# A planner's 1,870 priorities replaced, and its formula for matmul durations rewritten

## The chip, the core and the metric

The kernel runs on one core of a Trainium2 chip. The metric is the device time of one execution in microseconds (us); the time before is the median of three runs. A profile is one further execution, taken by the hardware profiler. "PE" is TensorE's matmuls, "PEld" its weight loads, "DVE" VectorE, "ACT" ScalarE, "POOL" GpSimd, "SP" the engine whose queue issues most of the DMAs.

## The reference, cut to what matters

The input `x` has 2048 rows and 512 columns. Two branches of it are mixed by a gate for each row:

```python
g = sigmoid((x * gate_w).sum(-1, keepdims=True))
a = irfft2(rfft2(x) * (w_r + 1j * w_i), s=(2048, 512))      # spectral filter
b = gelu(x @ w1 + b1) @ w2 + b2                             # 512 -> 1792 -> 512
return g * a + (1 - g) * b
```

All of it is in single precision.

## The kernel before, in words

Every matrix product is split for accuracy: an operand is rounded to a high part (`...h`, type fp32r) and a rest (`...l`), and a product is the sum of high by high, high by low and low by high. ACT makes most high parts, DVE subtracts to get the low parts, and PE runs the products.

The 2048 rows are 16 blocks of 128. `forward(j)` treats one block of the spectral branch: DVE folds the block (tiles `eo`, `cl`), ACT and DVE split it (`eoh`, `eol`), PE multiplies it with a table of cosines and sines (`pd`), ACT and DVE split what comes out (`x..h`, `x..l`), PE transforms along the rows of the block (`py`), and the result stays in SBUF as `y`. The PE steps of `pd` are runs of two matmuls: two with 260 columns for the high part and two with 130 columns for the low part (`prod`, lines 716 to 735). Butterflies between blocks (`radix4`), the filter (`filt`) and the way back (`stage4`, `inverse`) follow. In `inverse` the PE steps of `pz` mix matmuls of 256 and of 128 columns, and `pa` has runs of 256 columns.

The dense branch, `mlp(half, c)`, runs for two halves of the 14 groups of hidden units and four groups `c` of 512 rows: `up` gives `ph` (12 matmuls of 512 columns a step), ACT applies the gelu, the result is split (`g_..h`, `g_..l`), and `down` adds up `po` (3 matmuls a step, 512 columns, or 256 in the very last output group). This branch is 1,344 products of 512 columns, 33 of them divided into two of 256, and is most of PE's work.

Nothing in this program runs in the order in which the Python text names it. Every operation is first entered as a step of a `Graph` with its engine, a planned duration, a planned delay until its result is seen (`lag`), and a rank. `Graph.schedule()` (lines 219 to 339) then simulates the engines with these durations. Whenever an engine is free in that simulation, it takes, of the steps whose inputs are there and whose buffers can be had, the one with the lowest rank. It never leaves an engine idle because of a rank alone, with one exception: DVE and ACT may hold back up to 0.35 us for a step of lower rank that is about to be ready (`AHEAD`). Buffers of one class are handed out in a fixed sequence (`takes`, lines 244 to 255), whatever the ranks are. A PE step whose input comes from another engine is held back by another 0.4 us in the plan (`SPARE`, line 116). At most 8 DMAs of the SP queue (`hw`) and 3 of the POOL queue (`ring`) are under way at a time. The order that comes out is the order in which each engine's instructions are emitted, and each engine's instructions are executed in that order, with semaphores between engines. The planned times themselves are not used on the chip.

The ranks are a list of 1,870 numbers, `RANKS` (lines 342 to 452), in hundredths of a planned microsecond, one for each step: 470 on PE, 691 on DVE, 452 on ACT, 207 on the SP queue, 50 on the POOL queue. The planned duration of a PE step of `k` matmuls is `c_pe(n, k)` (line 494), where the caller gives the column count `n`.

The first PE step is `warm` (line 595 and after), eleven products of zeros before the data are there. The last steps are the second half's outputs for `c == 2`: `last` (lines 1164 to 1177) scales the last two `po` sums on DVE (line 1168), combines them with the spectral result (line 1173) and sends them off (line 1176). Just before it, `inverse(1, 1)` gives its result through `od` (line 999), `uv` (line 1002) and `y` (lines 1021 and 1024).

Of the kernel before, what the change touches and what calls it, by code (L numbers as in the profile page):

```python
# [172 lines left out]
class Graph:  # L173
# [282 lines left out]
def tile_kernel(ctx: ExitStack, tc: tile.TileContext, xt, w1, w2, b1, b2, x0g, wf, wrev, out, consts):  # L456
# [37 lines left out]
    def c_pe(n, k=1):  # L494
        return k * (n / 2400 + 0.0135) + 0.005
# [8 lines left out]
    def m(emit, n, k, reads, writes, rank=BULK):  # L504
        return add("pe", c_pe(n, k), 0.25, emit, reads, writes, rank)
# [785 lines left out]
```

## Time and profile before

| | |
|---|---|
| time, median of 3 runs | 372.75 us (372.29 to 372.97) |
| span of the profiled execution, first to last instruction | 370.8 us |
| PE busy | 365.1 us (98%), 1,838 matmuls |
| DVE busy | 327.5 us (88%), 691 instructions |
| ACT busy | 229.6 us (62%), 454 instructions |
| DMA moved | 62.99 MB |

The profiled execution's span is 1.95 us below the median time of the runs. What lies around the span, before the first and after the last instruction, is in the time of the runs and not in the span; the same 1.95 us is added wherever a span is turned into a time below.

A busy PE is an engine on which some matmul is under way; matmuls overlap, so that the duration of one is longer than the distance from its start to the start of the next. The pace of PE is read from those distances. "Idle before" is the time an engine stood still before an instruction, and the arrow names what ended it.

### The profile page before, as it was taken

What the parts mean: (1) busy time and instruction counts of PE and PEld (TensorE: products, weight loads), DVE (VectorE), ACT (ScalarE), POOL (GpSimd) and SP (SyncE); (2) the same over time, 40 slices, a digit from 0 to 9 for tenths busy, and PEclk for the clock granted to TensorE, in tenths of its full rate; (3) what the DMA queues carried; (4) which work ended last, traced back from release to release, by engine and by line L of the source; (5) the groups of instructions that cost most, each with busy time, mean ns of one, the idle gap of its engine ahead of it and who ended that gap; (6) DMA issues with size and microseconds to landing.
All of it is one profiled execution on the core that took longest, in us unless ns stands there. A gap on an engine that the chain in (4) does not pass through costs nothing.

```text
span 370.8 us, 5565 instructions
## 1 busy us (share of the span) xinstructions
PE 365.1 (98%) x1838; PEld 309.9 (84%) x1838; DVE 327.5 (88%) x691; ACT 229.6 (62%) x454; POOL 44.1 (12%) x54
## 2 busy tenths in 40 slices
PE   8999999999999999999999999999999999999995
PEld 6888888888888888888888888888888888888885
DVE  4999999999999789999999999588849696789996
ACT  5776587976678735375367213894697549457830
POOL 0000000000000002021032020001403222221031
PEclk9999999999999999999999999999999999999999
DMA  8962899425954216479289762318968999736268
GB/s 276 389 194 73 257 282 342 147 71 151 289 173 141 77 23 170 142 157 256 72 214 267 225 120 55 57 25 291 209 130 112 211 285 187 130 88 139 88 85 198
DMA packets 50868, 62.99 MB, mean 170 GB/s; under 512 B 4656, under 2 KB 31344, under 8 KB 50064
## 3 DMA queue, kind: packets, MB, share of 16 engines
q1 hardware_dynamic: 43496, 49.54, 41.3%
q0 software_dynamic: 7200, 12.85, 23.1%
q8 instruction: 14, 0.23, 0.2%
q10 hardware_dynamic: 144, 0.26, 0.2%
q14 instruction: 14, 0.11, 0.1%
HBM read 38.64 MB, written 23.73 MB: 168 GB/s over the span
## 4 chain that ended last, share of the span: by engine, by line
PE 95%; DVE 1%; DMA 1%; issue 0%; ACT 0%; SPq 0%; DVEq 0%
PE ph L530 41%; PE po L530 40%; PE pz L530 4%; PE pd L530 4%; PE py L530 3%; PE pa L530 3%; DMA xr<-in_xt 1%; DVE uv L1002 0%; DVE y L1021 0%; SPq L588 0%; DVE y L1024 0%; DVE mxl L650 0%; DVE o L1168 0%; ACT mxh L649 0%; ACT od L999 0%
## 5 line engine op out<-in xcount | busy, mean ns | idle before, releaser
L1106 ACT ACTIVATE ph<-ph,b1t 128x512 f32<-128x512 f32 x56 | 36.9, 659 | 41.5 <-PE ph L530 39.9
L949 ACT ACTIVATE sw<-y,al 64x512 f32<-64x512 f32 x32 | 23.0, 722 | 2.2 <-DVE y L812 1.6
L908 DVE TENSOR_TENSOR m<-y,wf 128x514 f32<-128x514 f32 x32 | 20.8, 689 | 0.2
L956 DVE SCALAR_TENSOR_TENSOR pq<-y,al,sw 128x256 f32<-128x256 f32 x32 | 14.4, 481 | 5.9 <-ACT sw L952 5.5
L521 POOL DMA_DIRECT2D bacc<-o x12 | 10.5, 877 | 73.2 <-ACT o L1155 60.2
L521 POOL DMA_DIRECT2D wa7l<-in_w x1 | 1.0, 1017 | 141.0 <-ACT wa7l L582 141.0
L1155 ACT ACTIVATE o<-po 128x512 f32<-128x512 f32 x12 | 7.1, 595 | 15.9 <-PE po L530 15.8
L1152 ACT ACTIVATE o<-po,b2t 128x512 f32<-128x512 f32 x16 | 10.7, 686 | 7.6 <-PE po L530 7.5
L1002 DVE TENSOR_TENSOR uv<-pa,od 128x512 f32<-128x512 f32 x16 | 10.6, 685 | 3.6 <-ACT od L999 3.5
L764 ACT ACTIVATE y<-pys 64x257 f32<-64x257 f32 x24 | 10.0, 418 | 5.2 <-DVE pys L761 4.8
L530 PE MATMUL pd<-cf,eoh 128*128 128x260 f32 x64 | 12.7, 285 | 0.0
L688 DVE TENSOR_TENSOR eo<-xr 128x256 f32<-128x256 f32 x30 | 12.0, 418 | 0.0
L530 PEld LDWEIGHTS pd<-cf,eoh 128*128 128x128 f32 x64 | 10.6, 189 | 1.5 <-issue 0.2
L999 ACT ACTIVATE od<-pa 128x512 f32<-128x512 f32 x8 | 4.8, 599 | 10.2 <-PE pa L530 9.9
L952 ACT ACTIVATE sw<-y 1x512 f32<-1x512 f32 x16 | 10.1, 629 | 0.4
L530 PE MATMUL pd<-cf,eol 128*128 128x130 f32 x64 | 10.3, 253 | 0.0
L702 DVE TENSOR_TENSOR xr<-eo 128x256 f32<-128x256 f32 x24 | 9.8, 418 | 0.1
L530 PEld LDWEIGHTS pd<-cf,eol 128*128 128x128 f32 x64 | 9.6, 189 | 0.1
L649 ACT ACTIVATE mxh<-xm 128x512 fp32r<-128x512 f32 x12 | 6.9, 623 | 3.7 <-PE ph L530 3.7
L650 DVE TENSOR_TENSOR mxl<-xm,mxh 128x512 fp32r<-128x512 f32 x12 | 7.8, 686 | 1.2 <-ACT mxh L649 1.2
L705 DVE TENSOR_TENSOR eol<-xr,eoh 128x512 fp32r<-128x512 f32 x12 | 8.3, 688 | 0.2
L1046 DVE SCALAR_TENSOR_TENSOR ba<-gb,ba 128x512 f32<-128x512 f32 x12 | 8.1, 685 | 0.3 <-DMA ba<-bacc 0.3
(713 smaller groups left out, 1353.6 us busy)
## 6 DMA issues: line engine op xcount, KB each, us to landing
wf<-in_wf SPq DMA_DIRECT2D x16, 257.0 KB, 4.9
bacc<-o SPq DMA_DIRECT2D x16, 256.0 KB, 3.3
xr<-in_xt SPq DMA_DIRECT2D x15, 256.0 KB, 3.5
war<-in_w SPq DMA_DIRECT2D x14, 256.0 KB, 3.5
wbr<-in_w SPq DMA_DIRECT2D x14, 256.0 KB, 3.5
xm<-in_xt SPq DMA_DIRECT2D x12, 256.0 KB, 4.3
bacc<-o POOLq DMA_DIRECT2D x12, 256.0 KB, 4.0
ba<-bacc SPq DMA_DIRECT2D x12, 256.0 KB, 3.2
```

The source lines that it names most:

```text
L521: return add("pool", kb / 150, 3.4, lambda: nc.gpsimd.dma_start(dst(), src(), accum_op=ALU.add), reads, writes, rank)
L530: pe.matmul(ps, w, x, start=start, stop=stop)
L688: v(lambda s=s, op=op: vec.tensor_tensor(eo.ap()[:, s], x.ap()[:, 0:2], x.ap()[:, 2:4], op=op), 256, [x], [(eo, s)], FEED)
L702: v(lambda k=k, op=op: vec.tensor_tensor(quarter(cl, k), eo.ap()[:, :, 0], eo.ap()[:, :, 1], op=op), 256, [eo], [(cl, k)] if j % 4 == 0 or ...
L764: a(lambda o=o, i=i: act.activation(Y[j].ap()[o:o + HP, 1], pys.ap()[i:i + HP, 1], AF.Copy), 257, [(pys, 1)], [(Y[j], 1 + k)], 0, more=0.1)
L908: v(lambda mk=mk, k=k, y=y, w=w: vec.tensor_tensor(mk.ap(), y.ap(), w.ap()[:, k:k + 1, :ND].to_broadcast([P, 2, ND]), op=ALU.mult), 514, [ ...
L949: a(lambda sw=sw, y=y, o=o, i=i: act.activation(sw.ap()[o:o + HP], y.ap()[i:i + HP, ::-1, :HD], AF.Copy, scale=al.ap()[i:i + HP, 0:1]), 51 ...
L952: a(lambda sw=sw, y=y, j=j: act.activation(sw.ap()[HP:HP + 1], y.ap()[HP:HP + 1, ::-1, :HD], AF.Copy, scale=math.cos(math.pi * j / NJ)), 5 ...
L956: v(lambda sw=sw, pq_=pq_, y=y, j=j, k=k, op=op: vec.scalar_tensor_tensor(pq_.ap()[:, k], y.ap()[:, k, :HD], al.ap()[:, 1 + j:2 + j], sw.a ...
L1002: v(lambda i=i, op=op: vec.tensor_tensor(uv.ap()[:, :, i], ps.ap()[:, 0], od.ap(), op=op), 512, [ps, od], [(uv, i)], 2)
L1106: a(lambda f=f, ps=ps: act.activation(ps.ap(), ps.ap(), AF.Gelu_apprx_tanh, bias=b1t.ap()[:, f:f + 1]), 600, [b1t], [ps], 0.9 if half else ...
L1152: a(lambda o=o, ps=ps, q=q: act.activation(o.ap(), ps.ap(), AF.Identity, scale=-1.0, bias=b2t.ap()[:, q:q + 1]), 600, [b2t, ps], [o])
```

## The change

`RANKS` gets 1,870 other numbers, and `c_pe` another formula. No step is added or removed, no step's instructions are changed, and buffers, their counts, the lags and the other engines' planned durations stay as they are. The order that `Graph.schedule()` works out from the new ranks and durations is a new one on all engines and queues, DMAs included.

```diff
 RANKS = (
-    -149, 43, 217, 3, 143, 100, 150, 574, 1118, 447, 437, 885, 624, 1856, 1001, 866, 832, 912, 1753, 1799, 1869, 396,
-    517, 392, 844, 2523, 2641, 2614, 2664, 2689, 2749, 3018, 2746, 2717, 2784, 3053, 2805, 2960, 3278, 3147, 3324, 3185,
...
+    1739, 333, 416, -261, 178, -1542, -1584, 475, 1315, 602, 458, 538, 1168, 2342, 1590, 1107, 826, 535, 1968, 1784,
+    176, -131, 337, 531, 413, 2156, 1355, 2523, 1971, 3144, 2922, 3104, 2217, 3743, 2290, 3175, 4410, 3095, 3289, 3239,
...
 )
...
     def c_pe(n, k=1):
-        return k * (n / 2400 + 0.0135) + 0.005
+        return k * max(n / 2400 + 0.0135, 0.112)
```

215 rows, old and new, of the table RANKS are left out of this document.

## The prediction

> **What bounds the kernel now.** I read the page first, then the busy time in stretches of 20 us, then the waits of PE, and last the starts of single matmuls.
>
> ```profile
> span 370.8 us, 5565 instructions
> PE 365.1 (98%) x1838; PEld 309.9 (84%) x1838; DVE 327.5 (88%) x691; ACT 229.6 (62%) x454; POOL 44.1 (12%) x54
> PE   8999999999999999999999999999999999999995
> DVE  4999999999999789999999999588849696789996
> ```
>
> PE is busy 365.1 of 370.8 us, and the tenths leave holes only in the first and the last slice. The columns of the next view are stretch and length, then PE, PEld, DVE, ACT and POOL busy, granted clock, DMA share, GB/s.
>
> ```profile
> 20.00:40.00 20.00, 20.00 (x108) 17.19 (x107) 19.45 (x45) 12.85 (x32) 0.00 (x0) 1.00 0.39 111
> 40.00:60.00 20.00, 20.00 (x117) 17.45 (x117) 19.43 (x50) 14.55 (x41) 0.00 (x0) 1.00 0.98 305
> 60.00:80.00 20.00, 20.00 (x112) 17.35 (x111) 19.21 (x49) 15.13 (x43) 0.00 (x0) 1.00 0.56 176
> 80.00:100.00 20.00, 20.00 (x112) 17.22 (x111) 19.70 (x45) 13.24 (x35) 0.00 (x0) 1.00 0.63 191
> 100.00:120.00 20.00, 20.00 (x106) 17.04 (x105) 19.42 (x44) 16.12 (x38) 0.00 (x0) 1.00 0.53 167
> 160.00:180.00 20.00, 20.00 (x90) 16.53 (x90) 19.89 (x43) 9.89 (x17) 4.17 (x5) 1.00 0.78 172
> 340.00:360.00 20.00, 20.00 (x111) 17.28 (x110) 19.13 (x37) 13.89 (x23) 4.38 (x5) 1.00 0.43 87
> ```
>
> PE is busy for 20.00 of 20.00 us throughout, at a granted clock of 1.00. The second thing to see is DVE: from 20 to 120 us it is idle 0.55 + 0.57 + 0.79 + 0.30 + 0.58 = 2.8 us in 100. Among PE's waits there is one row:
>
> ```profile
> PE none L530 <- DVE zero L593: 1.1, 1, 1.1
> ```
>
> A busy PE may still be slowed, because matmuls overlap in the records. So I take the pace from the starts:
>
> ```profile
> 9.48:366.40 356.92, 356.92 (x1805) 1.00 0.65 167
> 15.11 2.04 PE po L530 x9
> 114.84 1.08 PE py L530 x9
> 207.36 14.96 PE po L530 x66
> 294.86 1.43 PE pa L530 x12
> 360.77 0.97 PE pa L530 x8
> ...
> 41.20 0.48 PE L530 MATMUL pd<-cf,eoh 128*128 128x260 f32 x2
> 41.52 0.39 PE L530 MATMUL po<-g_5h,wb5h 128*128 128x512 f32 x1
> 42.33 0.34 PE L530 MATMUL pd<-cf,eol 128*128 128x130 f32 x2
> 42.50 0.45 PE L530 MATMUL po<-g_4h,wb4h 128*128 128x512 f32 x1
> 42.78 0.39 PE L530 MATMUL po<-g_4l,wb4h 128*128 128x512 f32 x1
> ```
>
> A 512-column matmul takes 14.96 / 66 = 0.2267 us; one of 256 to 260 takes 1.43 / 12 = 0.119 or 1.08 / 9 = 0.120. Two narrow ones and the wide one behind them take 42.78 - 42.33 = 0.45; less 0.227, a narrow one costs 0.112.
>
> By the code's loops, after the divided first `ph` step PE has 1,311 matmuls of 512 columns, 364 of 256 to 260 and 128 of 128 or 130. At those paces: 1,311 x 0.2267 + 364 x 0.120 + 128 x 0.112 = 297.2 + 43.7 + 14.3 = 355.2 us. The stretch from 9.48 to the end of the last matmul's share (its row, below, starts at 366.13; + 0.12 = 366.25) is 356.8 us. So at most 1.6 us of this long middle is lost. One piece of it is visible: the two 260-column matmuls from 41.20 took 0.32 to the next start, not 0.24.
>
> **The change part by part.** *The formula.* Its name promises longer durations for 128 and 130 columns. The smallest count that any caller passes is 240: the 130-column step calls with 240, the step that contains the 128-column ones with 256. At 240 the first term is 240 / 2400 + 0.0135 = 0.1135, already above 0.112. So the floor never binds. What does change is the 0.005 us a step that is gone: 470 PE steps, less the fixed warm-up, x 0.005 = 2.35 us of planned PE time. A run of 12 is planned at 2.722 instead of 2.727 (measured 12 x 0.2267 = 2.72), a `po` step at 0.6805 instead of 0.6855 (0.680), the 130-column pair at 0.227 instead of 0.232 (0.224). The plan comes nearer the chip by 5 ns a step. On the chip itself a planned duration costs nothing: 0.
>
> *PE's work.* Same matmuls, same runs inside each step. If the price of a matmul doesn't hang on its neighbours, 0. The two narrow ones always stand together, since one step emits both.
>
> The Trainium skill ("TensorE: Matmul & The Clock Gate", LDWEIGHTS) gives a load of 128 columns as columns / 1.2 ns, 107 ns; the 0.112 above agrees with it. The same page (Back-to-back issue gap) gives some 81 ns for sustained 128-column matmuls and 131 ns for 512; the 0.227 of this trace contradicts the second. By its first figure and an order that lets it show, 128 x (112 - 81) ns = 4.0 us would go; that is a rival below.
>
> *The start.* The divided `ph` step has 24 matmuls of 256 columns, 24 x 0.12 = 2.88 us, and lasts from 5.68 to 9.48:
>
> ```profile
> 5.68 0.53 PEld L530 LDWEIGHTS ph<-mxh,wa0h 128*128 128x128 f32 x4 [0.52 <-ACT mxh L649]
> 7.57 0.53 PEld L530 LDWEIGHTS ph<-mxh,wa0h 128*128 128x128 f32 x4 [0.30 <-ACT mxh L649]
> 8.90 0.54 PEld L530 LDWEIGHTS ph<-mxl,wa0h 128*128 128x128 f32 x4 [0.32 <-DVE mxl L650]
> 9.48 0.40 PE L530 MATMUL ph<-mxh,wa1h 128*128 128x512 f32 x1
> ```
>
> That is 0.92 us lost, in waits on the first splits. In the new list the first weight has -5.95 and the first three blocks of x have 1.78, -15.42 and -15.84. The blocks share a class and so must go in sequence, and the next weight stands at 2.07. The SP queue thus still begins with weight, x, x, x, weight. The tables `cf` and `tf` now go ahead of the second matrix's first weights (4.75 and 5.31 against 5.93; before, 5.74 and 3.92 against 2.50). Those are first needed by `po` at 15.1 us, so 5 us of wide `ph` matmuls cover the move; without that cover one issue later is about 0.5 us. I take 0, between -0.3 and +0.5.
>
> *The middle.* New ranks stand 8.4 us (root mean square) from the old ones, over all engines; loads, stores and splits trade places by as much. Nothing is added, so each instruction costs 0 in itself, and the whole effect is whether PE finds its inputs. Best case: the avoidable part of the 1.6 us goes; I leave 0.4 for edges between kinds of matmuls, so -1.2. Worst case, from DVE, the nearest to full: the work is hidden only so long as DVE delivers `eol`, `x..l` and `g_..l` in time. A 512-wide subtraction is spaced 1.29 / 2 = 0.645 us (`uv`, next fence), against 0.609 in the unchanged planning formula. Two of them put ahead of one that PE waits for make it 1.29 late; the plan keeps 0.4 in hand, so PE stands for 0.9. Three such places make +2.7. The plan that is nearer on PE should lose a little less: I take -0.2 from -1.2 to +2.7.
>
> DMAs move too:
>
> ```profile
> xm<-in_xt SPq DMA_DIRECT2D x12, 256.0 KB, 4.3
> ```
>
> The plan counts 256 / 300 + 2.5 = 3.35 us for it. A load put where the DMA share is 0.98 (40 to 60 us) could be late by the difference, 0.95, and with 0.4 in hand PE would lose 0.55 each time. The 8-deep SP list then fills and the next load is late too. I put this inside the +2.7, since a load that is late makes DVE late.
>
> *The end.*
>
> ```profile
> 362.40 1.29 DVE L1002 TENSOR_TENSOR uv<-pa,od 128x512 f32<-128x512 f32 x2
> 363.72 1.29 DVE L1021 TENSOR_TENSOR y<-uv 128x512 f32<-128x512 f32 x2
> 364.93 1.29 DVE L1024 TENSOR_TENSOR y<-y,ba 128x512 f32<-128x512 f32 x2
> 366.13 0.28 PE L530 MATMUL po<-g_13h,wb13l 128*128 128x256 f32 x1
> 366.13 0.75 DVE L1168 SCALAR_TENSOR_TENSOR o<-gb,po 128x256 f32<-128x256 f32 x2
> 366.80 0.75 DVE L1173 TENSOR_TENSOR o<-y,o 128x256 f32<-128x256 f32 x2
> 367.24 0.90 SPq L1176 DMA_DIRECT2D out<-o  x2
> ```
>
> From 362.40 DVE works without a hole to 367.55, so the end is DVE's, not PE's: it starts when `pa` of the last `inverse` is done. If that came earlier, PE's last matmul (366.41) would bound: 366.41 + 0.375 for its half of `o`, against 366.88. That is 0.1 on its row; with the second half's combination and issue no longer queued behind the first half's, up to 0.4. In the new list the last two `pa` steps (360.94, 363.38) stand ahead of the first steps of both final `po` sums (364.58, 373.54). In the old list (360.18, 361.86) one of those, at 361.37, went between: three matmuls, 0.36 us. Against it, the DVE step at line 1168 for the third output group moves from 361.39 to 367.67; if it finds no hole before `uv`, its 0.69 us falls into the tail, where something else has left. I take -0.2, between -0.4 and +0.4.
>
> **The sum.** 370.8 + 0 (PE's work) + 0 (start) - 0.2 (middle) - 0.2 (end) = 370.4 us of span. The profiled execution lies 1.95 us below the median of the runs, so 372.35, rounded to 372.4 us.
>
> **The rivals.**
>
> *A. The waits are recovered (faster).* A plan nearer to PE's real pace removes most of the 1.2 us of the middle, and the tail gives 0.4: 372.75 - 1.0 - 0.4 = 371.35 us. For it: the pieces exist (41.20). Against: they are small and scattered, so each must be hit. The limit of all gains together is 0.3 + 1.2 + 0.4 = 1.9 us, 370.85.
>
> *B. DVE becomes the bound of the forward stage (slower).* Place: 20 to 120 us, where DVE has 2.8 us idle in 100. It decides as soon as a split stands over 0.4 us later than planned. Price: three places of 0.9, 372.75 + 2.7 = 375.45; one place, 373.65. For it: DVE rows of 19.2 to 19.7 in 20, and a plan that takes 0.609 for what is spaced 0.645. Against: in the old order the same shortfall produced no recorded wait of PE.
>
> *C. Narrow matmuls become cheaper between wide ones.* 372.75 - 4.0 = 368.75. Against it: at 42.33 they already stand between wide ones, and cost 0.112.
>
> *D. The formula as named had decided.* Since no caller is under 240, only ranks and 5 ns act; had the floor acted on counts of 130, the pair would be planned at 0.224, as good as the 0.227 it gets. The time would be that of the forecast.
>
> **How the numbers follow.** Of this kernel, 0.2% (0.75 us, about the spread of the runs before) is what a measurement tells from no change: 372.0 to 373.5. No measurable change, 372.4 us, own range 371.9 to 373.5: 0.42, D in it. A: 0.26. B, with one place or more: 0.30. C: 0.02. So faster 0.28, same 0.42, slower 0.30. The range goes down to the limit of all gains, 370.85, and up to B's three places with the upper ends of start or tail, 375.45 + 0.5 = 375.95: 370.9 to 376.0. Outside remain C and more than three places.
>
> **What would show it.** PE's busy rows at 20.00 in 20 from 20 to 360 us with one wait in its list: PE's work is invariant and B is wrong. A wait of PE on `eol`, `x..l` or `mxl`, or a stretch of 20 us with less than 19.5: B. Runs of 66 at other than 0.2267, or narrow pairs not at 0.224: the paces hang on the order, and C or its opposite holds. A stretch from the end of `pa`'s last run to the end of the span below 8.8 us (here 370.8 - 360.77 - 0.97 = 9.1) shows the tail's part. I would be wrong above all if the waits after 9.48 grew by over 1 us without DVE being late.

## The result: slower, and the profile after

The changed kernel takes 374.54 us (median of 11 runs, 373.0 to 378.1), against 372.75 us for the kernel before in 11 runs (372.19 to 373.37). The ratio is 1.0056, with a 95% interval of 1.0032 to 1.0081. The forecast was "no measurable change"; the kernel became slower by 0.56% by this ratio, by 1.79 us (0.48%) by the medians. That is above the 373.5 us up to which the forecast counted a time as no change, and inside the whole range of 370.9 to 376.0.

The page of the changed kernel, its first line, the busy times and the tenths of PE:

```profile
span 372.7 us, 5567 instructions
PE 364.6 (98%) x1838; PEld 309.6 (83%) x1838; DVE 327.1 (88%) x691; ACT 228.4 (61%) x454; POOL 44.1 (12%) x54
PE   7999999999999999999998999999999999999995
```

The span grew by 1.95 us (370.79 to 372.74), the median by 1.79; a run's time lies 1.7 to 1.9 us above its own span in every run whose span is listed. PE's tenths show one new gap, an 8 in slice 22, and a first slice that is a tenth emptier. The stretches of 20 us of the changed kernel, with the columns of the prediction's view, say where:

```profile
20.00:40.00 20.00, 20.00 (x107) 17.17 (x106) 19.32 (x47) 12.16 (x31) 0.00 (x0) 1.00 0.39 115
...
180.00:200.00 20.00, 18.65 (x83) 15.10 (x82) 17.55 (x36) 10.04 (x18) 3.86 (x5) 1.00 0.62 138
200.00:220.00 20.00, 20.00 (x90) 16.55 (x89) 19.83 (x40) 8.51 (x15) 4.04 (x5) 1.00 0.80 222
300.00:320.00 20.00, 19.31 (x93) 15.97 (x92) 14.15 (x30) 14.47 (x25) 4.39 (x5) 1.00 0.88 215
```

PE's share of the forward stage is as full as before, in this first stretch and in the four up to 120 us, 20.00 each. Two stretches lost time: 180 to 200 us, where ACT, DVE and the bytes of the DMAs fell as well, and 300 to 320 us. The clock is 1.00 in all of them. The list of PE's waits has one row for each loss, and one more at the start (engine, what waited, what it waited for; us in total, times, longest):

```profile
PE ph L531 <- DVE g_9l L578: 1.4, 1, 1.4
PE none L531 <- DVE zero L594: 1.1, 1, 1.1
PE ph L531 <- ACT mxh L650: 0.9, 1, 0.9
PE ph L531 <- DMA mxl<-xs2l: 0.7, 1, 0.7
```

The same places as single matmuls (start, duration, instruction; in brackets the idle time before it and what ended it):

```profile
9.21 0.40 PE L531 MATMUL ph<-mxh,wa1h 128*128 128x512 f32 x1
...
196.90 0.39 PE L531 MATMUL po<-g_6h,wb6l 128*128 128x512 f32 x1
198.64 0.50 PE L531 MATMUL ph<-mxh,wa11h 128*128 128x512 f32 x1 [1.35 <-DVE g_9l L578]
...
306.80 0.39 PE L531 MATMUL ph<-mxh,wa7h 128*128 128x512 f32 x1
307.88 0.50 PE L531 MATMUL ph<-mxl,wa7h 128*128 128x512 f32 x1 [0.69 <-DMA mxl<-xs2l]
...
368.25 0.28 PE L531 MATMUL po<-g_13h,wb13l 128*128 128x256 f32 x1
```

From here on a *hole* is the distance from one start to the next, less the 0.227 us that a wide matmul takes. The first hole is 198.64 - 196.90 - 0.227 = 1.51 us, the second 307.88 - 306.80 - 0.227 = 0.85 us; after each, the next start comes 0.11 us later than the pace. That is 2.58 us together. The account of the whole span then is: the divided first step ends 9.48 - 9.21 = 0.27 us earlier; from there to the start of the last matmul 368.25 - 9.21 = 359.04 us pass, before 366.13 - 9.48 = 356.65, so 2.39 more; from that matmul to the end of the span 4.49 us instead of 4.66, 0.17 less. -0.27 + 2.39 - 0.17 = +1.95. Without the two holes the middle would be 2.39 - 2.58 = 0.19 us shorter than before.

**The hole at 197 us.** The chain that ended last leads back to a load, and so does that of the second hole (start, duration, what):

```profile
187.47 6.16 DMA wf<-in_wf
193.82 2.43 DVE m L909 x4
197.90 0.69 DVE g_9l L578
...
208.50 14.28 PE po L531 x63
...
297.06 10.77 DMA mxl<-xs2l
307.88 2.79 PE ph L531 x11
```

A filter block (`wf`, 257 KB) landed 6.16 us after its issue; the planner counts 257 / 300 + 2.5 = 3.36. On DVE, `g_9l` stands in the new order behind eleven instructions of filter work, the ones of this filter first. On ACT the gelu of the same hidden group stands behind the split of a block of `w2` (`wb10h`) that was late too. First the new order, then the old one, rows of ACT and DVE:

```profile
193.65 0.17 DVE L904 SCALAR_TENSOR_TENSOR wf<-wf,rev 128x4 f32<-128x4 f32 x1 [2.21 <-DMA wf<-in_wf]
193.73 2.50 DVE L909 TENSOR_TENSOR m<-y,wf 128x514 f32<-128x514 f32 x4
...
194.68 0.64 ACT L1070 ACTIVATE wb10h<-wbr 128x512 fp32r<-128x512 f32 x1 [5.32 <-DMA wbr<-in_w]
195.88 0.64 ACT L1107 ACTIVATE ph<-ph,b1t 128x512 f32<-128x512 f32 x1
196.56 0.60 ACT L577 ACTIVATE g_9h<-ph 128x512 fp32r<-128x512 f32 x1
```

```profile
191.09 0.16 DVE L903 SCALAR_TENSOR_TENSOR wf<-wf,rev 128x4 f32<-128x4 f32 x1
191.75 0.66 ACT L1106 ACTIVATE ph<-ph,b1t 128x512 f32<-128x512 f32 x1 [2.42 <-PE ph L530]
192.34 0.62 ACT L1069 ACTIVATE wb10h<-wbr 128x512 fp32r<-128x512 f32 x1
194.15 0.69 DVE L577 TENSOR_TENSOR g_9l<-ph,g_9h 128x512 fp32r<-128x512 f32 x1 [0.76 <-ACT g_9h L576]
```

Before, ACT ran the gelu (191.75) ahead of `wb10h` (192.34), and `g_9l` was ready at 194.84, 2.8 us ahead of the `ph` step that needs its PSUM buffer (197.67). After, ACT stood 5.32 us and DVE 2.21 us on loads, with that gelu and that subtraction queued behind. DVE then worked without idle time from 193.65 to 197.90, and only then came to `g_9l`; `g_9h` had been ready at 197.16. So in this execution the filter, through DVE, set the end of the hole; the late `w2` block, through ACT, would by itself have let `g_9l` start 0.74 us sooner, still too late for PE. The filter's load also had less time: in the kernel before it was issued at 185.97 and DVE came to it at 191.09, 5.1 us later, without a wait; in the changed kernel DVE was ready for it at 193.65 - 2.21 = 191.44, 4.0 us after its issue. In the planned times the slack between the end of `g_9l` and the start of that `ph` step shrank from 2.85 to 1.06 us.

**The hole at 307 us.** It is the reload of the third group of rows, two transfers of 1 MB (`mxh`, `mxl`). In the new order three `po` steps fewer stand between the issue and the first use. After: `mxl` issued at 297.06 and wanted by the second matmul of the step, at 306.80 + 0.23 = 307.03, 9.97 us later; it took 10.77. In the kernel before, two rows of the SP queue and of PE:

```profile
295.26 0.47 SPq L527 DMA_DIRECT2D mxl<-xs2l  x1
...
307.27 0.39 PE L530 MATMUL ph<-mxl,wa7h 128*128 128x512 f32 x1
```

And from the list of DMA issues between 290 and 300 us of the kernel before (last column: us from issue to landing):

```profile
mxl<-xs2l SPq DMA_DIRECT2D x1, 1024.0 KB, 10.8
```

It was wanted 307.27 - 295.26 = 12.01 us after its issue. The transfer took the same time; the *cover*, the time from the issue of a load to its first use, went from 12.0 to 10.0 us.

### The profile page after: what moved, and what is told of

It reads as the page before. It is cut to its first block, busy times and chain, and to the rows that moved or that the text cites. A ratio compares the mean times of both kernels' runs of the same rounds, so it can differ in the third digit from the quotient of the medians.

```text
span 372.7 us, 5567 instructions
## 1 busy us (share of the span) xinstructions
PE 364.6 (98%) x1838; PEld 309.6 (83%) x1838; DVE 327.1 (88%) x691; ACT 228.4 (61%) x454; POOL 44.1 (12%) x54
## 4 chain that ended last, share of the span: by engine, by line
PE 82%; DVE 9%; DMA 7%; issue 1%; ACT 0%; DVEq 0%; SPq 0%
PE ph L531 36%; PE po L531 32%; PE pz L531 4%; PE pd L531 4%; PE py L531 3%; DMA mxl<-xs2l 3%; DMA wf<-in_wf 3%; PE pa L531 3%; DVE m L909 2%; DVE y L813 1%; DMA xf<-in_x0g 1%; DVE y L911 0%; DVE uv L1003 0%; DVE y L1022 0%; DVE c1d L811 0%
## 5 line engine op out<-in xcount | busy, mean ns | idle before, releaser
L1153 ACT ACTIVATE o<-po,b2t 128x512 f32<-128x512 f32 x16 | 10.8, 687 | 12.8 <-PE po L531 12.2
L1000 ACT ACTIVATE od<-pa 128x512 f32<-128x512 f32 x8 | 4.8, 599 | 10.8 <-PE pa L531 10.7
L522 POOL DMA_DIRECT2D out<-ba x8 | 7.3, 911 | 8.6 <-DMA out<-y 4.2
```

Source lines behind the costliest of these rows:

```text
L522: return add("pool", kb / 150, 3.4, lambda: nc.gpsimd.dma_start(dst(), src(), accum_op=ALU.add), reads, writes, rank)
L1153: a(lambda o=o, ps=ps, q=q: act.activation(o.ap(), ps.ap(), AF.Identity, scale=-1.0, bias=b2t.ap()[:, q:q + 1]), 600, [b2t, ps], [o])
```

## The experiments

Every order below is that of the kernel named, with a few steps taken out of the finished list and put in elsewhere. The lines added after `order = g.schedule()` are always

```diff
+    def put(ns, at, late):
+        moved = [s for n in ns for s in order if s.n == n]
+        for s in moved:
+            order.remove(s)
+        i = [s.n for s in order].index(at) + late
+        order[i:i] = moved
```

where a step's number is its place in the `Graph` as entered, and `late` is 0 for ahead of step `at` and 1 for behind it. The table has all twelve runs, with the time against the kernel before on the same chip:

| run | made from | median us | ratio, 95% interval | span of its profile | holes over 0.2 us after 10 us |
|---|---|---|---|---|---|
| split_first | after | 375.02 | 1.0085 (1.0053 to 1.0117) | 373.4 | 1.23 at 201, 1.0 at the reload |
| reload_cover | after | 373.89 | 1.0026 (1.0010 to 1.0042) | 372.9 | 0.39 at 23, 1.47 at 197 |
| both_moves | after | 374.28 | 1.0032 (1.0019 to 1.0045) | 373.3 | 0.40 at 23, 0.88 at 197, 0.25 and 0.82 at 201 to 203 |
| before_less_cover | before | 374.62 | 1.0059 (1.0038 to 1.0080) | 372.5 | 1.48 at the reload |
| filter_early | after | 373.21 | 1.0021 (1.0008 to 1.0033) | 371.4 | 1.08 at the reload |
| filter_early_cover | after | 372.41 | 0.9991 (0.9978 to 1.0004) | 370.3 | 0.26 at 23 |
| old_ranks_new_formula | before | 374.11 | 1.0049 (1.0029 to 1.0069) | 372.3 | 1.04 at 115 |
| new_ranks_old_formula | after | 379.74 | 1.0184 (1.0169 to 1.0199) | 377.0 | 0.94 at 145, 1.08 at 194, 0.67 at 210, 0.58 at 218, 1.12 at the reload and smaller ones |
| three_moves | after | 372.22 | 0.9974 (0.9961 to 0.9987) | 370.7 | none |
| before_late_filter | before | 373.52 | 1.0024 (1.0014 to 1.0034) | 370.9 | none |
| gelu_first | after | 373.89 | 1.0043 (1.0019 to 1.0066) | 372.5 | 1.28 at the reload |
| gelu_and_split | after | 374.72 | 1.0054 (1.0034 to 1.0074) | 372.2 | 0.22 at 201, 1.54 at the reload |

### split_first: the filter's steps behind `g_9l` on DVE

```diff
+    put((1052, 1053, 1046, 1078, 1047, 1054), 1429, 1)
```

> The changed kernel with one move on DVE: the split g_9l (line 578) goes ahead of the six small filter steps (lines 904, 911, 913, 917) that stand before it, so it no longer waits behind all the work that a late filter load (wf) has held up. Theory T (two separate holes in PE, each a load that lands later than planned with too little work ahead of its consumer): the wait of PE on g_9l at about 197 us, 1.5 us in the profiled run, shrinks to under 0.3; the hole of 0.85 us at about 307 us stays; median 374.5 - 1.4 = about 373.1 us. Rival R (the whole order runs late, and a wait taken away here comes back at the next step): the span stays at about 372.7 us and the median at about 374.5, with another wait of PE within some 20 us.

Measured: 375.02 us. The hole at 197 us shrank from 1.51 to 0.11 (197.48 - 197.14 - 0.227), but a new one of 202.92 - 201.46 - 0.227 = 1.23 us opened one hidden group later:

```profile
196.73 0.69 DVE L578 TENSOR_TENSOR g_9l<-ph,g_9h 128x512 fp32r<-128x512 f32 x1 [2.78 <-ACT g_9h L577]
201.46 0.39 PE L531 MATMUL po<-g_7h,wb7l 128*128 128x512 f32 x1
202.18 0.69 DVE L578 TENSOR_TENSOR g_10l<-ph,g_10h 128x512 fp32r<-128x512 f32 x1
202.92 0.50 PE L531 MATMUL ph<-mxh,wa12h 128*128 128x512 f32 x1 [1.06 <-DVE g_10l L578]
```

DVE now stood 2.78 us idle for `g_9h`, which on ACT was still behind the late `wb10h`; then the six steps that I had moved ran ahead of `g_10l`. So the order on DVE alone isn't the cause: with DVE out of the way ACT's queue still made DVE late, and the work that had been put off was paid for at the next subtraction.

### reload_cover: the three `po` steps back ahead of the reloaded group

```diff
+    put((1653, 1654, 1655), 1781, 0)
```

> The changed kernel with one move on PE: three po steps (nine matmuls, 2.04 us) that follow the first ph step of the third group of rows go ahead of it, so that the reload of mxl (from xs2l) has 12.0 instead of 10.0 us from its issue to its first use. Theory T: the hole of 0.85 us at about 307 us is gone, the one at about 197 us stays; median about 373.7. Rival R: ph2_7 is now 2 us later, the gelu and what hangs on it are too, and PE stands somewhere in 310 to 330 us by as much; median about 374.5.

Measured: 373.89 us. The hole at 307 is gone, and PE works from 294.96 to the next stage without one; the hole at 197 is there as before (1.47), and a small one, 0.39, appears at 23 us. The ratio is 1.0026 where the changed kernel had 1.0056, which is 1.1 us, beside the 0.96 us that the hole and the late start after it cost in the profile; the two intervals overlap. The second mechanism is confirmed.

### both_moves

```diff
+    put((1052, 1053, 1046, 1078, 1047, 1054), 1429, 1)
+    put((1653, 1654, 1655), 1781, 0)
```

> Both moves. Theory T: no hole above 0.3 us after 10 us, span about 370.3, median 372.3 (the order's start is 0.25 us and its end 0.17 us shorter than before's), and the runs lie as close together as those of the kernel before (about 1 us) instead of over 5 us. Rival R: about 374.5, or other holes; spread as wide as now.

Measured: 374.28 us, not the time of the kernel before. The reload's hole is gone; at 197 to 203 us 0.88 + 0.25 + 0.82 = 1.95 us are lost in this execution. This confirms split_first: what was put behind `g_9l` came back at `g_10l`. It also shows ACT's part in the first hole. DVE stood on the filter as long as in the changed kernel, the six steps were out of the way, and `g_9l` then waited for ACT:

```profile
194.58 0.17 DVE L904 SCALAR_TENSOR_TENSOR wf<-wf,rev 128x4 f32<-128x4 f32 x1 [2.29 <-DMA wf<-in_wf]
197.80 0.69 DVE L578 TENSOR_TENSOR g_9l<-ph,g_9h 128x512 fp32r<-128x512 f32 x1 [0.64 <-ACT g_9h L577]
```

So ACT's queue alone still cost 0.88 of the 1.5 us.

### before_less_cover: the reverse, in the old order

Made from the kernel before: three `po` steps, with 2.04 us of PE, are put behind the first step that uses the reload.

```diff
+    put((1654, 1655, 1648), 1781, 1)
```

> The kernel before, with the reverse of the second move: three po steps go from ahead of the first ph step of the third group of rows to behind it, which takes 2.04 of the 11.9 us between the issue of the mxl reload and its first use. Theory T: PE stands about 0.9 us on that reload at about 305 us, median about 373.5 (0.2% slower), and the runs spread wider. Rival R (the old order as a whole is early enough): no wait, 372.75.

Measured: 374.62 us. The hole appears in the old order, where the new one had it:

```profile
304.94 0.39 PE L530 MATMUL ph<-mxh,wa7h 128*128 128x512 f32 x1
306.65 0.50 PE L530 MATMUL ph<-mxl,wa7h 128*128 128x512 f32 x1 [1.32 <-DMA mxl<-xs2l]
```

1.48 us in the profile and 1.77 us in the median, more than the 0.85 of the changed kernel: `mxl` was issued at 295.21 and wanted at 305.17, again 10.0 us, and was used only 11.4 us after its issue. Both the hole and the median are above the 0.9 us and 373.5 us expected. The cover is the cause; its price changes with the landing time of the execution.

### filter_early: three filter blocks loaded ahead of the burst

Six filter tiles get four buffers of the class `z`, and three of the loads are issued at 178 us. The order of ACT and of DVE isn't touched.

```diff
+    filters = [x for s in order for x in s.bufs if x.name in ("wf10", "wf14", "wf3", "wf7", "wf11", "wf15")]
+    for k, x in enumerate(dict.fromkeys(filters)):
+        x.tag, x.slot = "z", k % 4
+    put((1048, 1077, 1083), 909, 1)
```

> The changed kernel; six of the sixteen filter loads (wf10, wf14, wf3, wf7, wf11, wf15) get four buffers of tag z, which nothing else uses between 130 and 230 us, and three of them (wf14, wf3, wf7) go to the SP queue's free stretch at 178 us instead of 187 to 192. Moving one split on DVE had only passed the wait on from g_9l to g_10l, so the theory is now T2: DVE as a whole is some 2 us late after 191 us because a filter load cannot be issued until the buffer before it is read, lands after 6.2 us, and DVE stands 2.2 us on it. T2: DVE's wait on the late wf is gone, PE's hole at 197 to 203 us is under 0.3 us, the hole at 307 us stays (0.85 to 1.0); median 374.5 - 1.4 = 373.1. Rival R2 (DVE simply has too much planned ahead of g_9l, loads or not): PE still stands over 1 us on g_9l or g_10l; median 374.5.

Measured: 373.21 us; no hole at 197 to 203 us, and the reload's hole, 1.08, remains. The block of `w2` on which ACT stood shows why both queues were served. First its issue in the changed kernel (ACT began on it at 194.68, row above), then its issue and its use in this run:

```profile
188.11 0.56 SPq L1065 DMA_DIRECT2D wbr<-in_w  x1
```

```profile
186.84 0.34 SPq L1065 DMA_DIRECT2D wbr<-in_w  x1
190.79 0.63 ACT L1070 ACTIVATE wb10h<-wbr 128x512 fp32r<-128x512 f32 x1 [1.77 <-DMA wbr<-in_w]
```

With the filters out of these 8 us the block is issued 1.3 us earlier, with no filter load just ahead of it in the SP queue, and ACT has it 3.95 us after its issue instead of 6.57. ACT's stand on `wb10h` fell from 5.3 to 1.8 us and DVE's on `wf` from 4.3 to 2.2 in all. So the filter loads in this stretch are the common cause of both stands in the new order. Their number alone isn't: the kernel before issues three of them and three blocks of `w2` in the same 8 us (medians 6.2 and 5.3 us to landing, where the trace has the landing), and there the old order has no hole.

### filter_early_cover

```diff
+    # the lines of filter_early, and
+    put((1653, 1654, 1655), 1781, 0)
```

> The same, and the three po steps ahead of the first ph step of the third group of rows, as in the earlier run that took the hole at 307 us away. T2: no wait of PE over 0.3 us after 30 us; span 370.3 to 370.8, median 372.3 to 372.7, level with the kernel before or 0.1% faster. R2: 373.9, as with the second move alone.

Measured: 372.41 us, ratio 0.9991 (0.9978 to 1.0004), with a span of 370.3 us: the changed kernel without its two holes is as fast as the kernel before, no more. One hole of 0.26 us is left at 22.81, before `ph` on `g_3l`.

### old_ranks_new_formula: the formula alone

Made from the kernel before:

```diff
     def c_pe(n, k=1):
-        return k * (n / 2400 + 0.0135) + 0.005
+        return k * max(n / 2400 + 0.0135, 0.112)
```

> The kernel before with the new formula for PE durations alone; 39 of the 470 PE steps and 34 of the 691 DVE steps then stand at another place. If the 5 ns a step are without effect (the prediction), 372.75 within 0.75 us. If a plan in which PE is 2.35 us shorter takes time away from in front of PE's inputs everywhere (loads are planned as short as before), PE stands at one place or more and it is slower by 0.5 to 2 us.

Measured: 374.11 us, ratio 1.0049 (1.0029 to 1.0069). Five nanoseconds a step moved 39 of the 470 PE steps, 34 on DVE, 21 on ACT and 9 on SP to other places, and cost 1.2 us by the medians. That is the size of most of what the whole change costs, but not the same loss: the changed kernel has no hole at this place. The loss here is a hole of 1.04 us, in PE's rows of this run:

```profile
114.77 0.28 PE L530 MATMUL py<-x11l,tf 128*128 128x258 f32 x1
115.93 0.39 PE L530 MATMUL py<-x15h,tf 128*128 128x258 f32 x1 [0.88 <-ACT o L1152]
```

PE waited for ACT's `o`, which ran at 115.20 and stands in ACT's queue behind two table loads for the gate. These come later in this order. First this run, then the kernel before:

```profile
110.73 1.28 ACT L1195 ACT_TABLE_LOAD   x1
112.25 1.28 ACT L1198 ACT_TABLE_LOAD   x1
```

```profile
107.45 1.28 ACT L1195 ACT_TABLE_LOAD   x1
108.98 1.28 ACT L1198 ACT_TABLE_LOAD   x1
```

The order's own plan has a hole of 1.06 us at this point (114.79), so this isn't a surprise of the chip: the planner saw it, and had no rule to move back. Over the whole kernel the planned holes of PE are 0.39 us in the old plan and 1.63 with the old ranks and the new formula.

### new_ranks_old_formula: the ranks alone

```diff
     def c_pe(n, k=1):
-        return k * max(n / 2400 + 0.0135, 0.112)
+        return k * (n / 2400 + 0.0135) + 0.005
```

> The new ranks with the old formula. The ranks were not made for these durations and the plan has 5.2 us in which PE stands, at six places from 115 us on (before: 0.39). If the plan's own holes are real, the span is 370.3 + 4.8 = about 375 to 377 and the median 377 to 379; if a few ns a step don't matter and the ranks alone make the time, 374.5.

Measured: 379.74 us, ratio 1.0184 (1.0169 to 1.0199), above the 377 to 379 expected, with holes from 23 us on, the larger ones in the second half of the span. Its plan has 5.2 us of holes (0.99 at 145.7, 1.38 at 194.96, 1.23 at 218.04 and others), mostly at the places where the chip has them; the largest on the chip, 1.12 us at the reload, isn't in the plan. Each list of ranks fits the durations that it is used with here (1.66 us of planned holes for the pair of the change), and is worse with the other formula. The two halves of the change can't be added: +1.2 us for the formula, +6.9 for the ranks, +1.8 for both.

### three_moves: filter_early_cover, and `g_3l` ahead of a fold

```diff
+    # the lines of filter_early_cover, and
+    put((617,), 176, 0)
```

> The changed kernel with the earlier filter loads, the longer cover of the reload, and one more split (g_3l) moved ahead of one fold on DVE, for the hole of 0.27 us that is left at 22.8 us. If what is left over before's pace is only that hole, the span is 370.0 and the median 372.1, below the kernel before by 0.2% (372.88 in the last comparison). If the order's start (0.25 us) and end (0.17 us) were gains of one profiled run only, 372.4 to 372.9, no difference.

Measured: 372.22 us (371.54 to 372.86), the kernel before 372.76 beside it; ratio 0.9974 (0.9961 to 0.9987). No hole over 0.2 us is left after 10 us. The two stretches that had lost time:

```profile
180.00:200.00 20.00, 20.00 (x90) 16.57 (x89) 19.65 (x41) 12.49 (x21) 4.36 (x5) 1.00 0.75 179
300.00:320.00 20.00, 20.00 (x103) 17.04 (x101) 15.17 (x31) 16.38 (x28) 6.14 (x7) 1.00 0.89 197
```

This version is faster than both kernels, by 0.26% against the one before by the ratio, of which the interval leaves 0.13 to 0.39. Its 12 runs spread over 1.3 us; those of the changed kernel over 5.1. The gain is near what start and end gave in the changed kernel's profile, 0.27 + 0.17 us, but this version's own profile shows it elsewhere: the divided first step ends at 9.42, 0.06 us sooner than before, the middle up to the last matmul (365.81) is 0.26 shorter, and the tail is 0.2 longer. Nor does this profile test the third move. Of the five profiles in which the divided first step ends earliest (8.87 to 9.12), four have the hole at 23 us, with 0.26 to 0.40 us; the changed kernel, where it ends at 9.21, has no hole there even without this move.

### before_late_filter: the filter late in the old order

Made from the kernel before: the load of that filter is put behind two loads of `w2`.

```diff
+    put((1048,), 1446, 1)
```

> The kernel before with one filter load (wf14) issued behind two loads of w2, some 2.5 us later than now. DVE then stands 2 to 3 us on it at about 191 us, as in the changed kernel. If the old order has 2 us more between the split g_9l and the matmuls that need it, as its planned times say (195.4 against 197.7, in the new plan 196.2 against 196.7), PE's hole at 197 to 203 us stays under 0.8 us and the median under 373.6. If DVE being late is enough by itself, the hole is 1.2 to 1.5 us, as in the changed kernel, and the median 374.2.

Measured: 373.52 us, ratio 1.0024 (1.0014 to 1.0034), and no hole in its profile. DVE stood longer than in the changed kernel, and yet `g_9l` was in time:

```profile
194.12 0.17 DVE L903 SCALAR_TENSOR_TENSOR wf<-wf,rev 128x4 f32<-128x4 f32 x1 [3.26 <-DMA wf<-in_wf]
196.34 0.68 DVE L577 TENSOR_TENSOR g_9l<-ph,g_9h 128x512 fp32r<-128x512 f32 x1
```

In this execution 3.26 us of standing cost PE nothing, because in the old order 2.2 us of filter work stood ahead of `g_9l`, not 4.25, and 2.85 us of slack were planned. So here a late load was harmless by what was queued behind it. The 0.76 us of the median aren't explained by this profile, whose own run was the fastest of the ten; the slower runs have no profile, and this stays open.

### gelu_first and gelu_and_split: ACT's queue put right

gelu_first puts the split of `wb10` and what hangs on it behind that gelu; gelu_and_split adds the DVE move of split_first.

```diff
+    put((1435, 1436, 1437, 1458), 1428, 1)
```

> A second look at the changed kernel's trace shows a queue that the first theories left out: ACT stands 5.3 us, from 189.4 to 194.7, on the load of one block of w2 (wb10h, line 1070), and the gelu of ph_9, whose matmuls are done at 194.0, is behind it. Here the changed kernel has the two splits of wb10 (and the POOL load and the next SP load that hang on them) behind that gelu and its high part, as the old order has; DVE's order, with g_9l behind the six filter steps, stays. If ACT's queue makes the hole (theory Q), PE's hole at 197 to 203 us is under 0.4 us and the median about 373.1 (the hole at 307 us stays). If DVE, standing on wf, makes it alone (T2), g_9l still runs at 197.9, the hole is 1.2 to 1.5 us and the median 374.5. If both paths are as late, it lies between.

> The same, and g_9l ahead of the six filter steps on DVE, so that neither queue holds the split back. Q and T2 both: no hole over 0.4 us at 197 to 203 us, median about 373.1. If only the loads count, and whatever stands behind them is late in turn (rival R from the first call), a hole of about 1 us comes back on g_10l, median 374.5.

Measured: 373.89 and 374.72 us. Neither has a hole at 197 us; gelu_and_split has 0.22 at 201. But this doesn't settle ACT's part. In gelu_first's profile the filter landed almost in time:

```profile
191.71 0.17 DVE L904 SCALAR_TENSOR_TENSOR wf<-wf,rev 128x4 f32<-128x4 f32 x1 [0.27 <-DMA wf<-in_wf]
195.96 0.68 DVE L578 TENSOR_TENSOR g_9l<-ph,g_9h 128x512 fp32r<-128x512 f32 x1
```

DVE has the same 4.25 us of work between these two rows as in the changed kernel (195.96 - 191.71 and 197.90 - 193.65), so here the earlier filter, not the moved gelu, set `g_9l`. Both keep the reload's hole, at 1.28 and 1.54 us, and so stay slower than the kernel before; gelu_and_split isn't better than the changed kernel. With the filter as late as in the changed kernel, ACT's part alone is seen in both_moves (0.88 us); no run shows DVE's part alone.

## Why the prediction was wrong, point by point

**"On the chip itself a planned duration costs nothing: 0."** The sentence is true of the chip; what I made of it for the order failed. I had worked out that the floor of 0.112 never binds and that 5 ns a step go, and concluded that the plan that is nearer on PE "should lose a little less". old_ranks_new_formula shows the opposite: these 5 ns move 39 PE steps and cost 1.2 us. Rival D had the same mistake: it gave the formula no effect on the order. The planned durations decide which step is ready first, and in that run one choice that falls the other way puts a pair of table loads, 2.6 us of ACT, 3.3 us later, in front of what PE waits for. How much of the changed kernel's 1.79 us is the formula's stays open: that hole isn't in the changed kernel, and the two halves don't add.

**"PE's work: 0."** Right. The changed kernel's 63 wide matmuls from 208.50 take 14.28 / 63 = 0.2267 us, the same as before to four digits. Rival C (cheaper narrow matmuls) found nothing to support it: a narrow pair and the wide one behind it take 43.83 - 43.37 = 0.46 us in the changed kernel, 0.45 before. My 0.112 for one narrow matmul is an average, though: by the rows from 42.33 the pair itself takes 0.17 and the wide one behind it 0.28, 0.05 more than its pace. So the agreement that I named for it is that of an average. The 131 ns of the Trainium skill ("TensorE: Matmul & The Clock Gate", Back-to-back issue gap) for 512 columns don't show in the new order either.

**"The start: 0, between -0.3 and +0.5."** -0.27, inside its bounds. PE waited 0.86 us on `mxh` at 6.14 and still ended the divided step sooner. The four profiles of orders made from the kernel before have this end at 9.22 to 9.50 (mean 9.41), the ten made from the changed kernel at 8.87 to 9.42 (mean 9.14): the gain is there on average, and a single profile may not show it.

**"The middle: -0.2, from -1.2 to +2.7."** This is the step that failed: the bounds held, the value came out at +2.39. Without the two holes the scattered small losses gave -0.19, near the forecast, but nothing shows that the nearer plan is the reason. The term that was mis-sized is the one for DMAs. I had "late by 0.95" from a median of 4.3 us against 3.35 planned, "and with 0.4 in hand PE would lose 0.55 each time", and put it "inside the +2.7" as a price of rival B, with a centre of zero. What failed in it is the "0.4 in hand" as much as the lateness: the time in hand isn't a constant of the plan, but what the order leaves, 2.85 us at `g_9l` in the old one and 1.06 in the new one. Measured, the filter in the burst took 6.16 us, 2.8 over the plan, and the other filter load and the one block of `w2` issued there whose landings are recorded took 7.2 and 8.1; the reload took 10.77, where the plan counts 2 x 1024 / 300 + 2.5 = 9.3 us from the first of the two issues, or 9.0 from the second (297.06 - 296.69 = 0.37 later), with 10.0 us of cover. So each place cost 1.62 or 0.96 us, not 0.55, and together 2.58. A median over the whole kernel says little of a burst. The 12.0 us of cover that the old order gave the reload could have been read from the trace before, and nothing in the plan kept them.

**Rival B, "DVE becomes the bound of the forward stage".** Its sign was right; its place and its mechanism weren't. That two of its places at 0.9 us make 374.55, where 374.54 was measured, is luck: the holes cost 1.62 and 0.96, and start and end gave 0.44 back. Two of its signs were seen, a wait on `mxl` and a stretch with less than 19.5 (18.65), but here `mxl` is a load and no split of DVE. From 20 to 120 us PE is busy 20.00 in 20. DVE wasn't slow: in the place that counted it stood idle for 2.21 us on a load, with `g_9l` in line behind. I named as the decider that a split stands 0.4 us later than planned; here the subtraction came over 2 us late, because the load was late by 2.8 and everything behind it on DVE, and on ACT, was late with it.

**Rival A, the waits are recovered.** Not seen in the changed kernel. With its holes removed by hand (three_moves) the new order gains 0.54 us on the median, against the 1.4 that A gave it.

**"The end: -0.2, between -0.4 and +0.4."** -0.17, inside the bounds by luck. I had read from the ranks that no `po` step goes between the last two `pa` steps any more. It still does (the chain that ended last, changed kernel):

```profile
362.53 0.36 PE po L531 x3
362.89 0.97 PE pa L531 x8
```

From the end of `pa` to the end of the last DVE instruction 5.81 us pass in both kernels (361.74 to 367.55, 363.87 to 369.68). What differs is the rest, the last store: 3.06 us instead of 3.24, and it varies from 3.06 to 3.70 over the fourteen profiles, in both orders. A rank isn't yet a place in the order; the order has to be worked out.

**"Wrong above all if the waits after 9.48 grew by over 1 us without DVE being late."** This came true in part: PE's waits after that grew by 1.4 + 0.7 us. In the first, DVE was late, but through a load; in the second DVE had no part.

What is shown: the two holes and their rows, the reload's cover in both directions (reload_cover, before_less_cover), the filter loads as the common cause of the first hole (filter_early), that without both holes the time is that of the kernel before (filter_early_cover), and what the formula does to the old order. What is argued from rows: that DVE set the last 0.74 us of the first hole in the profiled execution. Open: the formula's part in the changed kernel's time, why the loads in the burst took that long, the spread of the changed kernel's runs, 5.1 us, of which only one is profiled, and the median of before_late_filter.

## What to carry to other kernels

With an order that is planned ahead, a planned duration is part of the program: 5 ns a step moved 39 PE steps and cost 0.5% in the old order, and a list of priorities is worth something only together with the durations that it was found with. A new plan isn't judged by its planned span (`Graph.schedule()` gives 371.75 us for the old order and 370.67 for the new one, which is slower on the chip) but by its slack at each load: for every load look up how long it took from issue to landing in this stretch (not its median over the kernel), and what stands behind the waiting instruction in its engine's queue. Where one engine's queue is put right and the load stays late, the loss turns up at the next step, as in split_first; moving the load (filter_early) or putting work ahead of its first use (reload_cover) removed it.

## What the runs showed of the hardware

Loads of one size landed very differently by what was in flight with them: ACT had the same block of `w2` (256 KB) 3.95 us after its issue in filter_early and 6.57 us after it in the changed kernel, where filter loads shared the stretch. The Trainium skill ("DMA: Bandwidth & Descriptors", Latency and other measured facts) gives the access time of HBM as 0.2 us on average and 2 us at high load; the 2.6 us between the two loads are more than the 1.8 between these figures, and no run here splits them further. The 1 MB reload behind its sister took 10.8 us in the profiles of both kernels, though all else around it had moved, and was used only 11.4 us after its issue in before_less_cover.
